# Talking-heads attention and a squared-ReLU feed-forward: the start's gathers on two queues, its loads at once

## The chip, the cores and the metric

One core of one Trainium2 chip. The metric is the device time of one execution in microseconds (us).

## The reference, cut to what matters

```python
scores = scale * np.matmul(q, k.transpose(0, 1, 3, 2))        # 8 batches, 12 heads, 448 x 448
scores = np.einsum('bhij,hg->bgij', scores, w_pre)            # mix the heads
attn = softmax(scores)
attn = np.einsum('bhij,hg->bgij', attn, w_post)               # mix them again
x = np.matmul(attn, v)  # -> 3584 x 768
h = np.maximum(x @ w_in, 0.0)
return h * h @ w_out                                          # 768 -> 2048 -> 768
```

## The kernel before

Scores of one batch are made in four blocks of queries. For each block TensorE writes scores to PSUM (`s_ps`), ScalarE and VectorE evict them to `S` (two buffers, so two blocks). To mix heads with a matmul, the heads must lie along the partitions: a DMA per *tile* of 10 queries gathers 120 rows of `S` into one of twelve `G` tiles. Two tiles are one **double step**: mix (`m_ps`), exponential and sum (`e_sb`, ScalarE), reciprocal (`rc`, VectorE), normalise (`d`, GpSimd), mix back and turn (`at_ps`). TensorE and GpSimd run in the order of the program; the order on the other engines is chosen when the kernel is built.

```python
LAG, AHEAD = 2, 10
gts = [work.tile([P, S], BF16, name=f"G{x}") for x in range(AHEAD + 2)]
for t in gts:
    nc.gpsimd.memset(t[0:OFF, :], 0.0)
...
def gather(k):
    ...
    nc.sync.dma_start(out=g[OFF:OFF + H * n, :], in_=Sb[(b, blk)][x:x + n, :, :])
...
Sb[(b, blk)] = work.tile([P, H, S], BF16, name="S", tag="S", bufs=2)
...
gathers_for(-1)                       # tiles 0 to 9
for n in range(NPAIR, 2 * NPAIR):
    score_pair(n)                     # scores of the second block
for f in loads.get(-1, []):
    f()
for ds in range(nd + LAG):            # one double step
    for i in (2 * ds, 2 * ds + 1):
        for f in loads.get(i, []):    # position i: loads issued by GpSimd
            f()
    ...
```

`w1` (eight loads), `w2` (eight), `v`, `q` and `k` come by DMA from GpSimd, which also converts f32 to bf16 on the way, each at a numbered *position*, two positions to a double step.

The softmax here doesn't subtract the row's maximum and nothing guards it: scores larger than these inputs give would overflow.

## Time and profile before

| | before |
|---|---|
| time, median of three | 623.73 us (622.62 to 626.54) |
| span of the profiled execution | 621.2 us |
| TensorE busy | 557.5 us, 90% |
| gathers | 360, all issued by SyncE |

### The profile page before, as it was taken

The page shows a single profiled execution, that of the slowest core. Times are in us where ns is not written, and L with a number is a line of the kernel's source. Part 1 is how long each engine was busy: PE and PEld are TensorE (multiplying, and loading weights), DVE is VectorE, ACT ScalarE, POOL GpSimd, SP SyncE. Part 2 cuts the span into 40 slices and gives each one's busy share as a digit, 9 for nine tenths or more (in the row PEclk, how much of TensorE's full clock was granted, in tenths as well). Part 3 has the DMA queues.
Part 4 walks back from the last instruction along what each step waited for, and adds up shares of the span by engine and source line. Part 5 has one row for each costly group of instructions (what it writes and reads, how often), then busy time and mean ns, then how long its engine had stood idle before and what let it go on. Part 6 is the DMA issues. An engine that isn't in the chain of part 4 may idle for free.

```text
span 621.2 us, 26855 instructions
## 1 busy us (share of the span) xinstructions
PE 557.5 (90%) x11154; PEld 316.3 (51%) x11154; DVE 431.4 (69%) x1111; ACT 395.7 (64%) x1196; POOL 401.6 (65%) x591
## 2 busy tenths in 40 slices
PE   5545886888899999999999989999999999999997
PEld 3223564654455555554555445554555555555554
DVE  3355997898698768876787768876887787765101
ACT  3445664756677865787568865786578767872320
POOL 8345757647547984699448964699458944893450
PEclk9655989799899999999999999999999999999999
DMA  8799889848945695468753885468544575431102
GB/s 111 127 188 191 139 144 201 132 86 138 190 96 108 105 150 137 110 114 147 152 123 77 136 145 120 112 104 147 140 111 86 86 159 123 88 64 53 39 12 78
DMA packets 90911, 74.10 MB, mean 119 GB/s; under 512 B 6309, under 2 KB 87717, under 8 KB 90789
## 3 DMA queue, kind: packets, MB, share of 16 engines
q1 hardware_dynamic: 51842, 49.57, 33.6%
q0 software_dynamic: 38816, 22.81, 29.0%
q8 instruction: 87, 1.43, 0.9%
q14 instruction: 36, 0.29, 0.1%
q10 hardware_dynamic: 130, 0.01, 0.0%
HBM read 45.63 MB, written 11.01 MB: 91 GB/s over the span
## 4 chain that ended last, share of the span: by engine, by line
PE 65%; POOL 9%; DVE 9%; DMA 6%; ACT 4%; issue 3%; SPq 2%; ACTq 0%; DVEq 0%; POOLq 0%
PE o_ps L267 22%; PE h_ps L234 18%; PE at_ps L368 7%; PE ot_ps L185 7%; DMA G<-S 5%; PE m_ps L337 5%; DVE at L373 4%; POOL d L346 4%; PE s_ps L309 3%; PE tr_ps L162 3%; POOL h L246 3%; SPq L328 2%; DVE S L312 2%; ACT xt L196 1%; ACT e_sb L342 1%
## 5 line engine op out<-in xcount | busy, mean ns | idle before, releaser
L346 POOL TENSOR_SCALAR d<-e_sb,rc 128x448 bf16<-128x448 f32 x360 | 227.2, 643 | 180.0 <-DVE rc L344 178.2
L373 DVE CAST at<-at_ps 112x480 bf16<-112x480 f32 x360 | 219.4, 649 | 46.7 <-PE at_ps L368 43.2
L342 ACT ACTIVATE e_sb<-m_ps 128x448 f32<-128x448 f32 x360 | 195.7, 557 | 25.8 <-PE m_ps L337 12.6
L234 PE MATMUL h_ps<-xt,w 128*128 128x448 bf16 (+2 forms) x960 | 164.4, 319 | 3.2 <-DVE at L373 1.6
L267 PE MATMUL o_ps<-w,h 128*128 128x384 bf16 (+1 forms) x1024 | 162.5, 329 | 0.9 <-ACT xt L196 0.5
L312 ACT CAST S<-s_ps 128x448 bf16<-128x448 f32 x192 | 99.9, 541 | 91.4 <-PE s_ps L309 65.8
L312 DVE CAST S<-s_ps 128x448 bf16<-128x448 f32 x192 | 115.2, 613 | 22.2 <-DMA G<-S 20.1
L234 PEld LDWEIGHTS <-w 128*128 128x128 bf16 x960 | 80.4, 99 | 80.4 <-issue 30.8
L246 POOL TENSOR_TENSOR h<-hr 128x448 bf16<-128x448 f32 (+2 forms) x124 | 109.0, 887 | 17.2 <-ACT hr L244 17.2
L267 PEld LDWEIGHTS <-h 128*128 128x128 bf16 (+1 forms) x1024 | 82.9, 101 | 73.2 <-issue 27.8
L368 PE MATMUL at_ps<-post,d 60*64 60x60 bf16 x5760 | 87.6, 197 | 17.1 <-POOL d L346 9.8
L337 PE MATMUL m_ps<-G,pre 64*64 64x448 bf16 x720 | 79.0, 367 | 22.5 <-ACT S L312 9.6
L368 PEld LDWEIGHTS <-d 60*64 60x64 bf16 x5760 | 65.2, 111 | 61.1 <-issue 24.9
L244 ACT ACTIVATE hr<-h_ps 128x448 f32<-128x448 f32 (+2 forms) x136 | 68.7, 511 | 27.1 <-PE h_ps L234 12.2
L342 ACT ACTIVATION_READ_ACCUMULATOR e_sb<-m_ps 128x1 f32 x360 | 77.8, 216 | 0.0
L344 DVE RECIPROCAL rc<-sm 128x1 f32<-128x1 f32 x360 | 50.2, 155 | 37.3 <-ACT e_sb L342 35.4
L196 ACT ACTIVATE xt<-ot_ps,bvec 128x160 bf16<-128x160 f32 (+3 forms) x144 | 44.7, 384 | 49.2 <-PE ot_ps L185 37.7
L309 PE MATMUL s_ps<-kT,qT 64*64 64x448 bf16 x768 | 70.5, 375 | 0.8
L185 PE MATMUL ot_ps<-at,v 112*64 112x160 bf16 (+4 forms) x1152 | 48.6, 238 | 6.8 <-ACT S L312 4.0
L274 DVE COPY osb<-o_ps 128x384 f32<-128x384 f32 x48 | 25.9, 546 | 40.5 <-PE o_ps L267 40.4
L185 PEld LDWEIGHTS <-v 112*64 112x64 bf16 x1152 | 41.0, 114 | 19.7 <-issue 19.2
L337 PEld LDWEIGHTS <-pre 64*64 64x64 bf16 x720 | 28.0, 109 | 40.6 <-issue 35.1
(39 smaller groups left out, 215.1 us busy)
## 6 DMA issues: line engine op xcount, KB each, us to landing
G<-S SPq DMA_DIRECT2D x352, 105.0 KB
kst<-in_k_dram POOLq DMA_DIRECT2D x24, 224.0 KB, 5.8
qst<-in_q_dram POOLq DMA_DIRECT2D x24, 224.0 KB, 5.3
v<-in_v_dram POOLq DMA_DIRECT2D x24, 224.0 KB, 6.0
w<-in_moe_w_in_dram POOLq DMA_DIRECT2D x8, 384.0 KB, 10.5
w<-in_moe_w_out_dram POOLq DMA_DIRECT2D x8, 384.0 KB, 7.6
out_dram<-osb SPq DMA_DIRECT2D x8, 336.0 KB
out_dram<-osb SPq DMA_DIRECT2D x8, 288.0 KB
```

The costliest lines, as they stand in the source:

```text
L185: nc.tensor.matmul(ps[64 * hh:64 * hh + 64, TW * y + c0:TW * y + 2 + n], lhsT=vs[b][0:PR, g, r, :], rhs=at[0:PR, r, g, c0:2 + n], start=(y ...
L234: nc.tensor.matmul(ps[:, 0:n], lhsT=w1[ft // 4][:, c2, ft % 4 * 128:ft % 4 * 128 + 128], rhs=xts[b][:, c2, c0:c1], start=(c2 == 0), stop=( ...
L244: nc.scalar.activation(out=hr[:, 0:n], in_=ps[:, 0:n], func=ACT.Relu)
L246: square.tensor_tensor(out=h2ts[(b, ft)][:, c0:c1], in0=hr[:, 0:n], in1=hr[:, 0:n], op=ALU.mult)
L267: nc.tensor.matmul(dst, lhsT=h2ts[(b, ft)][:, mt * 128:mt * 128 + ROWS[mt]], rhs=w2[ft // 4][:, ft % 4, n2 * 384:(n2 + 1) * 384], start=(f ...
L309: nc.tensor.matmul(pss[hh][z:z + 64, 0:S], lhsT=qTs[b][rs, p, q0:q0 + 64], rhs=kTs[b][rs, p, :], start=True, stop=True)
L312: copy(out=Sb[(b, blk)][:, 2 * p + hh, :], in_=pss[hh][:, 0:S])
L337: nc.tensor.matmul(pss[y][64 * x:64 * x + 64, 0:S], lhsT=pre[rows, :], rhs=gs[x][rows, :], start=True, stop=True)
L342: nc.scalar.activation(out=e[:, :], in_=pss[y][:, 0:S], func=ACT.Exp, scale=SCALE, accum_out=sm[:, 0:1])
L346: nc.gpsimd.tensor_scalar(out=d[:, 0:S], in0=e[:, :], scalar1=rc[:, 0:1], scalar2=-1.0 / S, op0=ALU.mult, op1=ALU.add)
L368: nc.tensor.matmul(us[x][z:z + 64, c:c + HR], lhsT=d[rows, PR * r + z:PR * r + z + 64], rhs=post[rows, :], start=True, stop=True)
L373: nc.vector.tensor_copy(out=dst, in_=src)
```

## The change

Its intent: issue the first batch's gathers in half the time, have w1 and v loaded before the gathers need the DMA engines, and get the zero fills off GpSimd so that it can issue those loads earlier. The loads of the second batch's q and k and of w2 move up into the room that w1 leaves.

```diff
-        nc.gpsimd.memset(t[0:OFF, :], 0.0)
+        nc.vector.memset(t[0:OFF, :], 0.0)
...
-        nc.sync.dma_start(out=g[OFF:OFF + H * n, :], in_=Sb[(b, blk)][x:x + n, :, :])
+        eng = nc.scalar if b == 0 and k % 2 else nc.sync
+        eng.dma_start(out=g[OFF:OFF + H * n, :], in_=Sb[(b, blk)][x:x + n, :, :])
...
-        for x in range(8):
-            at_load(2 + 2 * (x // 2), load_w1, x)
-            at_load(28 + 2 * x, load_w2, x)
+        for x in range(2):
+            at_load(-1, load_w1, x)
         for x in range(3):
             at_load(-1, load_v, 0, x)
             at_load(44 + x, load_v, 1, x)
+        for x in range(2, 8):
+            at_load(-1, load_w1, x)
+        for x in range(8):
+            at_load(18 + 2 * x, load_w2, x)
         for x in range(6):
-            at_load(14 + 2 * x, load_qk, 1, x)
+            at_load(6 + 2 * x, load_qk, 1, x)
             at_load(46 + 2 * x, load_qk, 2, x)
```

## The prediction

> **What bounds the kernel now.** I read the page's slices first, then the stretches of the start, the chain of waits from 14 to 50 us in order of time, the waits of the same window, and last the trace's DMA packets counted by microsecond. The slices tell where there is time to gain:
>
> ```profile
> PE   5545886888899999999999989999999999999997
> PEclk9655989799899999999999999999999999999999
> DMA  8799889848945695468753885468544575431102
> ```
>
> One slice is 15.5 us. From the eighth on TensorE is nearly always busy, and 95% or more of it from 160 us to 560 us; the change touches nothing there. The first four slices (0 to 62 us) have it half idle at half clock, while the DMA engines are 70 to 90% busy. So the start is the place, and what the start loses or gains is passed on to the end about one for one, since what follows is a full TensorE queue in fixed order.
>
> ```profile
> core 0: us, PE busy (x) PEld busy (x) DVE busy (x) ACT busy (x) POOL busy (x), PEclk, DMA share, GB/s
> 12.00:18.00 6.00, 5.78 (x76) 3.34 (x72) 5.25 (x10) 5.25 (x13) 1.78 (x3) 1.00 0.90 115
> 18.00:26.00 8.00, 4.33 (x54) 1.51 (x52) 3.29 (x10) 3.42 (x12) 3.02 (x5) 0.61 0.56 108
> 26.00:37.00 11.00, 1.23 (x36) 0.68 (x37) 0.49 (x3) 1.22 (x5) 3.14 (x5) 0.50 1.05 180
> 37.00:43.00 6.00, 3.98 (x86) 1.99 (x85) 5.62 (x15) 4.52 (x14) 4.76 (x7) 0.50 0.80 175
> 43.00:54.00 11.00, 4.89 (x131) 2.60 (x133) 6.46 (x19) 4.61 (x16) 6.54 (x11) 0.50 1.13 199
> ```
>
> The third column after the stretch's length is VectorE's, then ScalarE's. Two stretches are nearly dead on every engine (26 to 37 and, in its second half, 43 to 54), and both have the DMA share over 1. Before the first is one with DMA at about half (18 to 26). The chain of waits says who holds whom:
>
> ```profile
> 26.88 1.32 SPq L328
> ...
> 28.38 8.52 DMA G<-S
> 36.90 1.14 DVE S L312 x2
> ...
> 43.82 4.03 DMA G<-S
> ...
> 48.38 4.67 issue
> ```
>
> ```profile
> ACT S L312 <- DMA G<-S: 14.7, 2, 9.8
> DVE S L312 <- DMA G<-S: 13.8, 2, 10.1
> ```
>
> From 17.29 to 28.2 us the chain is SyncE's queue issuing twelve gathers one after the other, 0.77 to 1.32 us each, 11 us in all. Then 8.5 us for gathers to land. The engines waiting are the two that evict scores into S: S has two buffers, so the third block's scores can't be written before all twelve gathers of the first block have left it, and with eight PSUM banks TensorE soon stops too. The second hole (48.4 to 53.3) is the same wait one block later; the 4.67 us that the chain calls "issue" stand beside waits of ACT and DVE that the second view books on the gathers.
>
> Why the gathers are slow to land: the eight loads of w1 (384 KB each) are issued by GpSimd between 24.1 and 42.4 us, into the middle of them. Counted by microsecond, gathers alone move 120 to 157 packets of 896 B (one gather is 120 packets). As w1 comes in, this falls to 28 to 45 a microsecond (26 to 30 us), then 75 to 83 (31 to 37 us), beside some 150 packets of w1. The last gather of the first block, issued at 26.88, lands at 36.8. Meanwhile the queue of loads carried nothing from 18.1 to 25 us, nor for about 1 us at 12 us.
>
> **What the Trainium skill says.** "DMA: Bandwidth & Descriptors", section "Queues, rings and completion order": each DMA engine goes round between the queue rows that have work, a packet at a time, and SyncE and ScalarE have a row each. The trace agrees in that gathers under a load fall to a third or two thirds of their rate, not to nothing. It follows, if it holds, that gathers in two rows get two turns to the load's one. The same page, "Issuing engines are not separate DMA queues", says that a second issuer only saves its sequencer's issue time. Here that time is 0.77 to 1.32 us a gather, which is not small: 11 us of the chain. Which of the two sections describes the gain is open; the kernel before has no run with both rows busy. "VectorE: DVE Perf Modes", "Zero memsets can be issued as uint32 (trn2)": half as many elements for bf16 zeros. The trace agrees in form (pre, 128x64 bf16, is filled as 128x32 uint32 in 85 ns).
>
> **The change part by part.**
>
> 1. The twelve zero fills leave GpSimd, where they stand from 6.18 to 11.18 us (461 ns each, 5.0 us in all). On VectorE as 224 words each I estimate 0.25 us each, 3 us in all, from the 85 ns of a 32-word fill and about 1 ns a word. VectorE is idle 2.06 us before 3.50, 1.33 us before 5.73 and again before its first copy at 7.03. So this costs 0 to 0.3 us on the path, and it frees GpSimd at 6.2.
>
> 2. The w1 and v loads are issued at once. GpSimd begins at about 6.7 instead of 11.7 and 24.1 us. They follow q and k in one queue, which still has these in flight until 11.4, so q and k aren't delayed and the gap at 12 us closes. Amount: w1 3072 packets of 1024 B, at about 165 a microsecond 18.6 us; v 1344 packets of 512 B, at 350 a microsecond 3.8 us. From 11.4 that would end at 34 us alone; with gathers between them I take 35 to 36. In the kernel before w1 ends at about 53. GpSimd will wait for load slots (eight semaphores in rotation) until about 19 us, which is harmless: its first d is at 22.95.
>
> The price: the first gathers, which now run on free engines (first landing about 20.3), run beside v and w1 from the start. At 45 packets a microsecond in each of two rows, about 90 in all, twelve gathers (1440 packets) take 16 us from 16.6, so they land at about 32.5 and not at 36.8. With one row at the later rate of 80, the number is nearly the same, 34.5.
>
> 3. Odd gathers of the first batch go to ScalarE: 22 of them. The first five will stand among its evictions of S at 17 to 19 us; five issues at 0.8 us delay either them or the first exponential (22.0) by 1 to 4 us, I take 2. This lies before the landing of the twelfth gather and so costs nothing extra at the first hole. Later one such issue falls in each step of two tiles. From 60 to 85 us ScalarE is busy 15.6 of 25 us and VectorE 22.8; seven issues of 0.78 add 5.5 us to ScalarE's queue, 84%. It does not become the bound, but its exponentials start later: I take 1.5 us lost.
>
> 4. The loads of q and k for the second batch start 8 positions (four double steps) earlier, those of w2 ten positions earlier. The former now fall into 33 to 45 us instead of 48 to 67, light packets at half the queue's rate. The latter leave the stretch before 101 us, where they were followed at once by v and k and by a gather that stands 6.09 us on the chain (102.27 to 108.36).
>
> Sum. The fourth pair of tiles (m_ps at 37.45) moves to about 33: 4.5 us. The second hole has no w1 any more and two rows: of its 4.7 us I count 4. GpSimd's two w1 issues that stand on the chain at 38.84 (1.5 us) go, and a q or k load comes near: 0.5. At 102 us I count 2 of the 6.09. Less 1.5 for ScalarE. Total 4.5 + 4 + 0.5 + 2 - 1.5 = 9.5 us; I round to 10, which gives 613.7.
>
> **Rivals.**
>
> Rival A, the holes vanish: gathers in two rows run at close to their lone rate, the twelfth lands by 27 us, each double step takes the 2.3 us that it takes between 37.5 and 49, and the eleventh pair, now at 60.86, comes at 47 to 48. With the 2 us at 102 that is 14 to 16 us, or 608 to 610. For it: round turns a packet at a time. Against it: 3.8 MB of loads are in front of the same engines, and the DMA share was over 1 whenever holes occurred.
>
> Rival B, the contention is only moved: the skill's second section is all there is, w1 holds the first gathers as it now holds the later ones, and the first exponential comes at 26 instead of 22. The twelfth gather lands at 35; only the second hole closes. Gain 4 to 6 us, 618 to 620. For it: the fall to 28 to 45 packets as soon as w1 starts.
>
> Rival C, ScalarE becomes the bound: its queue is in order, a gather there waits for S, for a free G and for an earlier gather's semaphore, and everything behind it waits too. If each of 17 later issues holds the exponentials for its whole 0.8 us and no slack takes it up, 13 us are lost and the change is worth nothing: 621 to 628. Against it: a double step takes 2.3 us at the least and some 4 us after 60 us, and the results of an exponential are used two double steps later.
>
> **Range and chances.** My sum lies between A and B. I give A about 0.3, the middle 0.4, B 0.2, C 0.1. Faster by over 2% means under 611.3 us: most of A and a part of the middle, 0.35. Slower by over 2% would take C and a worse schedule of all that follows: 0.03. The range 605 to 621 should hold it 8 times in 10.
>
> **What would show it right or wrong.** Right: the load queue shows no gap from 4 to about 35 us; the hole from 26 to 37 shrinks to under 5 us; that at 48 us is gone; step 3's matmuls stand near 33 us and the first h_ps (62.95) near 53; from 160 us on all stands the same distance earlier. ScalarE's waits on the gathers tell B from A: several microseconds before 35 us and none after would be my middle. It is wrong if first-batch exponentials wait behind ScalarE's DMA issues with TensorE idle after 60 us (C), if q and k land later than 11.4 us, or if TensorE's idle time after 110 us changes by more than 3 us: then the reordered queues, not the loads, would have moved the time.

## More of the kernel before

Columns: out<-in, issuing engine, count, size, median from issue to landing.

```profile
G<-S SPq DMA_DIRECT2D x352, 105.0 KB
kst<-in_k_dram POOLq DMA_DIRECT2D x24, 224.0 KB, 5.8
w<-in_moe_w_in_dram POOLq DMA_DIRECT2D x8, 384.0 KB, 10.5
w<-in_moe_w_out_dram POOLq DMA_DIRECT2D x8, 384.0 KB, 7.6
```

A gather is small against any of the loads, but the loads only have to arrive some time, and a gather has work waiting.

## The result, and the profile after

616.14 us (median of four, 614.33 to 617.23) against 625.13 us before (median of four). Ratios here and below are the mean time of one kernel's fast runs over that of the kernel before in the same rounds, so not quite the ratio of the medians; this one is 0.9854, interval 0.9804 to 0.9904. A second measurement gave 0.9865. So it is 8 to 9 us faster, under 2%, within the range and near the predicted 613.7.

The slices of the changed kernel, to be laid under those of before:

```profile
PE   5456888799799999999999899999999999999997
PEclk9655999999899999999999999999999999999999
DMA  9989958859645885488545875478543565431102
```

The first four slices are no fuller on TensorE than before. Loads stand in the first two slices of the DMA row (9, 9 for 8, 7), as intended, but the start did not get short. The same stretches as in the prediction, now of the changed kernel:

```profile
12.00:18.00 6.00, 5.62 (x70) 2.77 (x69) 5.03 (x10) 3.93 (x8) 2.75 (x5) 1.00 1.31 195
18.00:26.00 8.00, 1.31 (x12) 0.38 (x9) 1.77 (x4) 1.67 (x4) 1.26 (x2) 0.72 1.24 229
26.00:37.00 11.00, 4.52 (x88) 2.04 (x84) 3.70 (x12) 5.17 (x18) 3.10 (x5) 0.50 0.94 202
37.00:43.00 6.00, 4.63 (x118) 2.21 (x118) 5.59 (x17) 4.74 (x16) 5.89 (x10) 0.50 0.88 158
43.00:54.00 11.00, 5.62 (x124) 2.51 (x124) 6.08 (x16) 5.22 (x17) 6.11 (x11) 0.50 1.09 182
```

The hole from 26 to 37 is smaller (TensorE 4.52 us busy for 1.23), but there is a new one from 18 to 26 (1.31 for 4.33), where DMA went from a share of 0.56 to 1.24. One hole was traded for another. ScalarE's stream in order of time shows what the new hole is made of, first in the kernel before:

```profile
14.56 4.47 ACT L312 CAST S<-s_ps 128x448 bf16<-128x448 f32 x10
22.01 0.54 ACT L342 ACTIVATE e_sb<-m_ps 128x448 f32<-128x448 f32 x1 [2.98 <-PE m_ps L337]
```

and in the changed kernel:

```profile
14.62 2.28 ACT L312 CAST S<-s_ps 128x448 bf16<-128x448 f32 x5
16.68 7.61 ACTq L329 DMA_DIRECT2D G<-S  x5
24.33 2.28 ACT L312 CAST S<-s_ps 128x448 bf16<-128x448 f32 x5 [7.43 <-PE m_ps L338]
26.45 0.60 ACT L343 ACTIVATE e_sb<-m_ps 128x448 f32<-128x448 f32 x1
...
27.58 0.80 ACTq L329 DMA_DIRECT2D G<-S  x1
```

In the kernel before, ten evictions of S follow each other from 14.56 to 19.03 and the first exponential is at 22.01. Now five gathers stand among them and take 7.61 us, not 5 times 0.8: four are issued by 20.1, and the fifth has to wait for the semaphore of ScalarE's first gather, which lands at 23.5. The other five evictions, the exponentials and the twelfth gather (27.58) wait behind it. (The view books the 7.43 us before the evictions on a matmul; the fifth issue ends at 24.29, and they begin at 24.33.)

```profile
16.68 7.00 DMA G<-S
...
24.35 2.26 ACT S L312 x5
26.61 0.97 ACT e_sb L343 x4
27.58 6.93 DMA G<-S
...
46.88 3.80 DMA G<-S
```

Those are the chain's long pieces of the changed kernel. The first gather takes 7 us to land, the twelfth another 7, and the second hole is still there, at 46.88. The waits from 16 to 62 us say the same (for 14.7 and 13.8 before):

```profile
ACT S L312 <- DMA G<-S: 9.7, 2, 5.1
...
DVE S L312 <- DMA G<-S: 7.7, 2, 4.3
```

The best single ruler is the start of the first exponential of each double step, since all kernels here do the same work in the same order of steps. In us from the span's start, two profiles of the changed kernel:

```
double step      0      3      8     12     22     23     24     35     60
before       22.01  38.14  54.14  65.04  97.99 100.49 108.85 145.56 215.41
changed      26.45  36.96  52.19  63.08  95.74  98.07 101.31 137.88 207.62
changed (2)  27.04  38.00  53.18  64.07  96.74  99.07 102.31 138.90 206.43
```

The whole start is worth 2.25 and 1.25 us (double step 22). The gain is at one place: from double step 23 to 24 took 8.4 us and takes 3.2, and over the stretch from 22 to 35, 47.6 us become 42.1. After that the kernels run alike: from step 60 to 179, 350 to 352 us. Both profiles of the changed kernel give back some 2 us there (352.4 and 352.2 for 350.1), and both have one window of 3.4 us at half clock, at 352.5 and 351.2 us; of the other profiles only one has such a window (ScalarE's gathers alone, the second profile, 351.9 us).

### The profile page after: what moved, and what is told of

Its sections match the earlier page's. It is cut to its first block, busy times and chain, and to the rows that moved or that the text cites. A ratio compares the mean times of both kernels' runs of the same rounds, so it can differ in the third digit from the quotient of the medians.

```text
span 615.4 us, 26843 instructions
## 1 busy us (share of the span) xinstructions
PE 556.6 (90%) x11154; PEld 313.2 (51%) x11154; DVE 434.4 (71%) x1123; ACT 396.1 (64%) x1196; POOL 397.8 (65%) x579
## 4 chain that ended last, share of the span: by engine, by line
PE 63%; POOL 11%; DVE 11%; DMA 6%; ACT 5%; issue 3%; ACTq 0%; DVEq 0%; POOLq 0%; SPq 0%
PE o_ps L267 22%; PE h_ps L234 17%; PE at_ps L369 7%; PE ot_ps L185 6%; POOL d L347 5%; DVE at L374 5%; DMA G<-S 5%; PE m_ps L338 4%; POOL h L246 3%; PE s_ps L309 3%; PE tr_ps L162 3%; ACT e_sb L343 2%; ACT xt L196 2%; DVE S L312 1%; DVE h L246 1%
## 5 line engine op out<-in xcount | busy, mean ns | idle before, releaser
L374 DVE CAST at<-at_ps 112x480 bf16<-112x480 f32 x360 | 219.5, 649 | 44.9 <-PE at_ps L369 40.8
L234 PEld LDWEIGHTS <-w 128*128 128x128 bf16 x960 | 79.2, 98 | 79.9 <-issue 30.9
L274 DVE COPY osb<-o_ps 128x384 f32<-128x384 f32 x48 | 26.0, 546 | 40.5 <-PE o_ps L267 40.4
L185 PE MATMUL ot_ps<-at,v 112*64 112x160 bf16 (+4 forms) x1152 | 47.3, 234 | 2.8 <-DVE at L374 2.8
L338 PEld LDWEIGHTS <-pre 64*64 64x64 bf16 x720 | 27.9, 108 | 35.5 <-issue 26.5
```

The costliest lines, as they stand in the source:

```text
L185: nc.tensor.matmul(ps[64 * hh:64 * hh + 64, TW * y + c0:TW * y + 2 + n], lhsT=vs[b][0:PR, g, r, :], rhs=at[0:PR, r, g, c0:2 + n], start=(y ...
L234: nc.tensor.matmul(ps[:, 0:n], lhsT=w1[ft // 4][:, c2, ft % 4 * 128:ft % 4 * 128 + 128], rhs=xts[b][:, c2, c0:c1], start=(c2 == 0), stop=( ...
L338: nc.tensor.matmul(pss[y][64 * x:64 * x + 64, 0:S], lhsT=pre[rows, :], rhs=gs[x][rows, :], start=True, stop=True)
L374: nc.vector.tensor_copy(out=dst, in_=src)
```

## The experiments

Twelve runs. The stretches of the ruler for all kernels come after the single runs.

### Putting w2 back in the changed kernel

```diff
-            at_load(18 + 2 * x, load_w2, x)
+            at_load(28 + 2 * x, load_w2, x)
```

> The kernel after, with w2's loads put back ten positions, where the kernel before has them. Theory 1 (most of the gain is not at the start but at 102 us, because w2 is out of the way of v, k, q and the second batch's gathers): the exponential of double step 23 stays near 98 us, that of double step 24 goes from 101 back to 106 or later, and the time is 5 us longer, about 621 us. Rival (the hole at 102 us closes because gathers come earlier against their use, wherever w2 is): double step 24 stays near 101 to 103 and the time at 615 to 617.

619.75 us, ratio 0.9913 (0.9839 to 0.9986). The hole came back: step 23 to 24 takes 7.99 us. The start was 2.4 us better than in the changed kernel (step 23 at 95.7; expected 98), so step 24 was at 103.7 and not 106. Theory 1 holds; the interval of the time alone overlaps that of the changed kernel.

### w2's place alone, on the kernel before

```diff
-            at_load(28 + 2 * x, load_w2, x)
+            at_load(18 + 2 * x, load_w2, x)
```

> The kernel before with w2's loads ten positions earlier, nothing else. If w2's place is worth about nothing in sum (its earlier loads cost at 55 to 85 us what they save at 102 us, as the kernel after with w2 put back suggests: 2.4 us ahead at double step 23, 2.4 us behind at 24, equal at the end): 623 to 626. If the hole at 102 us is a loss by itself: 617 to 620, with double step 24 about 3 us after double step 23 instead of 8.4.

618.13 us, ratio 0.9902 (0.9834 to 0.9971). Step 22 at 97.78 (before 97.99), step 23 to 24 in 3.24 us, step 35 at 139.87 (before 145.56). So a change of one number gives 5 to 6 us, most of what the whole change gives. From step 12 to 22 it costs 0.6 us. How it acts is seen in the stretches around the hole, first before, then this kernel (columns as in the prediction):

```profile
96.00:100.00 4.00, 2.95 (x92) 2.31 (x95) 4.00 (x13) 3.10 (x11) 3.26 (x6) 1.00 1.03 223
100.00:104.00 4.00, 3.26 (x84) 2.25 (x78) 3.50 (x11) 1.62 (x6) 3.97 (x7) 1.00 1.10 209
104.00:110.00 6.00, 1.57 (x26) 1.47 (x27) 1.69 (x4) 1.58 (x6) 2.39 (x5) 0.88 1.20 201
```

```profile
96.00:100.00 4.00, 3.34 (x98) 2.50 (x98) 4.00 (x12) 2.95 (x11) 2.56 (x5) 1.00 0.53 115
100.00:104.00 4.00, 2.94 (x65) 2.23 (x66) 3.97 (x14) 2.64 (x8) 3.94 (x7) 1.00 0.98 132
104.00:110.00 6.00, 5.66 (x158) 4.28 (x158) 5.57 (x17) 5.32 (x20) 5.75 (x9) 1.00 1.22 193
```

From 96 to 100 us w2 still moves in the first (DMA share 1.03), and the last packets of gathers issued then start 6 to 7 us after the issue; the hole follows at 104. In the second only gathers move (0.53), their last packets start about 3 us after the issue, so they are ahead when v, k and q arrive at the same share of 1.22, and nothing stops.

### ScalarE's gathers alone, on the kernel before

```diff
-        nc.sync.dma_start(out=g[OFF:OFF + H * n, :], ...)
+        eng = nc.scalar if b == 0 and k % 2 else nc.sync
+        eng.dma_start(out=g[OFF:OFF + H * n, :], ...)
```

> The kernel before with the odd gathers of the first batch on ScalarE, nothing else. If issue time is what they save: the twelve gathers are issued in about 6 us instead of 11, before w1 begins at 24, so the twelfth lands at 27 to 30 instead of 36, double step 3 is at 32 to 34 instead of 38, the later holes stay, and the time is 3 to 5 us shorter, 619 to 622. If w1 governs all: double step 3 stays at 37 to 38 and the time at 624 to 626.

> ScalarE's gathers alone on the kernel before, once more in five rounds. If the moved loads add nothing to what ScalarE's gathers give: within 2 us of the changed kernel of the same call, ratio 0.984 to 0.990. If the loads carry a part of the gain that adds up: 3 us or more slower than the changed kernel.

615.55 us, ratio 0.9873 (0.9783 to 0.9963), and in five rounds 618.24 us, 0.9898 (0.9860 to 0.9936). Double step 3 at 30.6 and 30.9, better than expected, and step 22 at 90.7 and 90.8: 7.2 us ahead of the kernel before, where the changed kernel, which has this part too, is 1 to 2 ahead. The later hole stays (9.4 and 10.2 us). So the moved loads take away some 5 us of what ScalarE's gathers give at the start and add 5 or more at 102 us. The time of the repeated run is between its two predictions, 2.8 us behind the changed kernel, and the intervals overlap.

It also shows what two issuers are worth. SyncE alone issues gathers at 0.77 to 1.3 us each; two at a time need 0.83 to 1.55 us each here, and up to 2.3 in another run. In the changed kernel, where no gather has moved yet, two at a time need 0.77 to 0.85. The twelfth gather was issued at 23.4 us for 26.9 before, not in half the time, and landed at 27.1 for 36.8. A part of this may be w1's doing: its first load also comes 2.3 us later here (26.4 for 24.1), as GpSimd issues it after its first normalisations.

### All gathers on SyncE, in the changed kernel

```diff
-        eng = nc.scalar if b == 0 and k % 2 else nc.sync
+        eng = nc.sync
```

> The kernel after, all gathers from SyncE again, one row. Theory 2 (two rows give gathers two turns to the load's one, and this is what keeps the start from being worse): gathers move some 64 to 83 packets a microsecond instead of 128 beside w1, the twelfth lands at 38 us or later instead of 34.4, double step 3 starts at 40 instead of 37, and the time is 3 to 5 us longer, 619 to 621. Rival (ScalarE's queue is what hurts the start: its evictions of S stand behind its gathers until 24.3, so the first exponential is at 26.5 instead of 22.0): without them the first exponential is at 24 or earlier, double step 3 at 36 or earlier, and the time is 613 to 615.

616.89 us, ratio 0.9893 (0.9826 to 0.9961). Beside w1, gathers move 80 to 85 packets a microsecond with one row; the changed kernel moves 60 to 68 in each of two, some 127. So theory 2 is right about the rows, and double step 3 is at 40.8 as it said. But only 4 us lie between the two at step 3 and 0.8 at step 22: without ScalarE's gathers its evictions are not held up (first exponential at 24.9 for 26.5), and the second hole is 4.1 us for 7.2. The time fits neither reading, and it doesn't tell the two kernels apart. With w1 in front of the gathers it hardly matters who issues them.

### w1 and v at once alone, on the kernel before

```diff
+        nc.vector.memset(t[0:OFF, :], 0.0)      # for nc.gpsimd.memset
...
-        for x in range(8):
-            at_load(2 + 2 * (x // 2), load_w1, x)
+        for x in range(8):                       # v's three loads after the second
+            at_load(-1, load_w1, x)
```

> The kernel before with v and all of w1 loaded at once behind q and k and the fills on VectorE; gathers, second batch's q and k, and w2 as before. If w1 at once is worth something by itself (it closes the holes at 28 and 48 us): double step 3 at 36 to 39 us, double step 8 at 49 to 51 instead of 54.1, time 617 to 620. If it only moves the contention onto the first gathers: double step 3 at 40 to 41 as with one row and all loads moved, double step 8 at 52 to 54, and the time within 2 us of the kernel before.

620.12 us, ratio 0.9952 (0.9873 to 1.0032). Step 3 is later than before (40.3 for 38.1), as the second reading said, and the second hole is gone (step 7 to 8 in 2.3 us for 6.9), as the first said: 3.6 us ahead at step 22. In the changed kernel that hole is back (7.2 and 6.8 us). What stands in the load queue there, from 47 to 50 us, is q and k of the second batch at 276 to 287 packets a microsecond, and the gathers are down to 26 to 70. This kernel, with q and k in their old place, has none of them until 50. The kernel with all gathers on SyncE is a control for this: until step 8 it differs from this one in the place of q and k alone (its first w2 load is issued at 55.3 us). Its hole is 4.1 us for 2.3, and its step 8 is 2.5 us later. So q and k early cost some 2 us, in one profile of each. They are not the whole of the hole. The other 3 us come with ScalarE's gathers, and kernels that have these gathers with q and k in the old place have a hole of 4.9 to 5.8 us as well (ScalarE's gathers alone, w1 spread). In part this is only that ScalarE's gathers bring step 7 forward by 4.0 us and step 8 by 0.9; the rest stays open.

### w1 back in its old place, all else as changed

```diff
-            at_load(-1, load_w1, x)              # two, then v, then six
+            at_load(2 + 2 * (x // 2), load_w1, x)
```

> The kernel after, w1's loads back where the kernel before has them (v stays, q, k and w2 stay early, ScalarE's gathers stay). Theory 3 (w1 at once puts some 4 us of loads in front of the very first gathers and so costs the start what it saves later): first gather lands near 20 instead of 23.3, first exponential at 22 to 23, the twelfth gather at 27 to 29, double step 3 at 30 to 32 instead of 37; then w1 meets the second block's gathers together with q and k, and of these 5 to 6 us some 2 to 4 are given back; time 611 to 615. Rival (w1 at once is what helps): double step 8 later than in the kernel after (52.2), time 619 or more.

615.25 us, ratio 0.9852 (0.9785 to 0.9918). The first gather lands at 19.8 us and step 3 is at 30.5, as theory 3 says; the first exponential is at 24.1, later than the 22 to 23 expected. The give-back is at the upper end of what was expected: w1, q and k come together, steps 3 to 7 take 16.1 us (8.1 and 8.4 in the changed kernel), and of the 6.4 us gained at step 3 3.9 are given back by step 8, at 49.6. Step 22 is at 93.2. That is 2.6 to 3.6 us ahead of the changed kernel in the profile; the times don't tell the two apart.

One count separates kernels with all of w1 in front from the rest. From the issue of the first gather to the first packet of any gather:

```
w1 all in front:  changed 4.20, 4.15   w2 back 4.18   all on SyncE 4.18   w1 alone 4.17 us
w1 later:         before 1.50   w2 early 1.50   ScalarE alone 1.49, 1.49   w1 back 1.50   w2 early, ScalarE 1.50 us
two of w1 only:   the spread version below 1.95, 1.92   ScalarE from tile 11 1.49 us
```

In the first row v's loads, behind two of w1's, are also still moving, until 20.0 to 20.3 us. In the kernel before they move until 18.8 and its first gather is not held up, so v alone is not the reason. By what path w1 delays a packet in another queue row, the runs don't show.

### w2 early and ScalarE's gathers on the kernel before

```diff
+        eng = nc.scalar if b == 0 and k % 2 else nc.sync
...
-            at_load(28 + 2 * x, load_w2, x)
+            at_load(18 + 2 * x, load_w2, x)
```

> ScalarE's gathers and w2's earlier place on the kernel before, w1, q and k as before. ScalarE's gathers alone left double step 23 at 93.1 and double step 24 at 102.5, a hole of 9.4 us. If w2 in front of v and k makes this hole, it falls to about 3.5 us and the time is 610 to 613. If the earlier w2 delays the start as much, double step 23 is at 96 or later and the time stays at 614 to 617.

618.02 us, ratio 0.9913 (0.9839 to 0.9986): both readings missed. The hole at 102 us closes as expected (3.24 us), but step 22 is at 101.5, later than before. The profiled execution is the slowest of the four (622.39 us). Until double step 7 this kernel does the same as ScalarE's gathers alone and is still 4 us later, since in this execution issues of two queues at once took 2.3 us each; that part is chance. The rest is not: from step 12 to 22, 40.8 us for 34.8 with ScalarE's gathers alone. GpSimd now issues w2 between q's and k's loads while w1 is still coming, and each of those loads takes 14 to 19 us to land. The chain stands on the last of q's: it is issued at 66.05 us (57.7 with ScalarE's gathers alone), TensorE's turns wait for it, and it lands 16.93 us later. Two gains that each hold alone didn't add up, because w1, q, k and w2 stand in one queue in the order of issue.

### w1 spread over the double steps

```diff
+        eng = nc.scalar if b == 0 and k % 2 else nc.sync      # fills on VectorE too
...
         for x in range(3):
             at_load(-1, load_v, 0, x)
+        for x in range(2):
+            at_load(-1, load_w1, x)
+        for x in range(2, 8):
+            at_load(2 * x - 2, load_w1, x)                    # one to a double step
+        for x in range(8):
+            at_load(26 + 2 * x, load_w2, x)                   # 28 before
```

> ScalarE's gathers, fills on VectorE, v and two of w1's loads at once, the other six one per double step, w2 one double step earlier than before. With ScalarE's gathers alone the chain from 25 to 37 us is GpSimd: per double step 1.25 us of d and 1.5 us of issuing two loads. With one issue of 0.75 the step falls from 2.8 to about 2.1 us: double step 6 at 36.5 instead of 38.6 and no later than that at 8 (43), time 611 to 613. If instead the bytes of w1 set the pace there, double step 6 stays at 38 to 39 and the time at 614 to 616.

> ScalarE's gathers with w1 spread over the double steps, once more in five rounds. If w1 at once costs the start 3 us (double step 3 at 31.8 instead of 37.0 in the profiles): 2 to 4 us faster than the changed kernel, 611 to 614. If the profile of 610 us was a lucky execution: 614 to 617, as the changed kernel.

612.57 us, ratio 0.9840 (0.9756 to 0.9924), then 611.51 us, 0.9811 (0.9782 to 0.9840) in five rounds, where the changed kernel had 615.44 us, 0.9865 (0.9830 to 0.9900). It beats both: 4 us faster than the changed kernel and 12.6 faster than the one before (624.11 us in those rounds), which is 1.9%, with an interval that reaches past 2%. The two intervals just overlap; each profile is 6.5 us or more ahead at step 22. Step 6 is at 37.7 and 37.2, short of the 36.5 expected, and step 8 is at 45.9 and 45.4 for the expected 43; steps 3 to 7 take 8.3 and 8.5 us, for 9.6 and 11.0 with ScalarE's gathers alone. Step 22 is at 89.2 and 89.0, 9 us ahead of the kernel before, and the hole at 102 us is 4.4 and 4.6. The same stretches for its second profile:

```profile
18.00:26.00 8.00, 2.42 (x10) 0.73 (x9) 1.75 (x4) 3.06 (x8) 0.00 (x0) 0.59 0.68 168
26.00:37.00 11.00, 8.23 (x202) 4.08 (x202) 8.82 (x26) 8.09 (x27) 10.04 (x15) 0.50 0.88 157
...
43.00:54.00 11.00, 7.52 (x166) 5.33 (x165) 5.41 (x15) 6.76 (x22) 3.94 (x7) 0.52 1.06 191
```

From 26 to 37 TensorE does 8.23 us of work for 4.52 in the changed kernel, at a lower DMA share.

### The changed kernel again

> The changed kernel once more, five rounds, beside the next three on the same chip. Single executions of one kernel differ by 3 to 7 us, so the partial kernels' medians of four (615 to 620) can't be told apart yet. Expected 615 to 617, ratio 0.984 to 0.988, if the first result was typical.

615.44 us, ratio 0.9865, as expected.

### ScalarE only from the eleventh tile on

```diff
-        eng = nc.scalar if b == 0 and k % 2 else nc.sync
+        eng = nc.scalar if b == 0 and k % 2 and k >= 10 else nc.sync
...
-            at_load(2 * x - 2, load_w1, x)      # against the spread version
+            at_load(2 + 2 * x, load_w1, x)
-            at_load(14 + 2 * x, load_qk, 1, x)
+            at_load(18 + 2 * x, load_qk, 1, x)
-            at_load(26 + 2 * x, load_w2, x)
+            at_load(28 + 2 * x, load_w2, x)
```

> As the spread version, but ScalarE takes odd gathers only from the eleventh tile on, so that its first evictions of S and exponentials are not behind gathers, and the six later loads of w1 start two double steps later, q and k of the second batch two later. If ScalarE's queue order costs the first steps 2 to 3 us: first exponential at 22 instead of 25.5, double step 3 at 28 to 30, time 608 to 611. If the start is set by landing gathers anyway: double step 3 at 31 to 33 and the time as the spread version's, 611 to 614; if the later q and k then meet the turns of the second batch, longer.

621.09 us, ratio 0.9930 (0.9896 to 0.9964), a miss. The first exponential is at 22.8, so ScalarE's queue does cost the first steps some 2 us. Step 3 is at 32.05 all the same: its chain is SyncE's serial issue again, then the landing.

```profile
25.74 0.95 SPq L329
...
26.74 4.02 DMA G<-S
```

With w2 at its old place the hole at 102 us is 8.9 us, and q, two double steps later, is waited for by the turns of the second batch. It loses by those, more than by what it tried.

### All kernels on one ruler

First exponential of double steps 3 and 22, and stretches between them, in us:

```
                        step 3  7 to 8  step 22  23 to 24  22 to 35   ratio
before                   38.14    6.94    97.99      8.36     47.57
w1 and v at once         40.26    2.32    94.40      7.63     46.43   0.9952
ScalarE's gathers        30.55    4.92    90.74      9.44     47.88   0.9873
   again                 30.89    4.99    90.80     10.16     48.75   0.9898
changed, w2 back         36.55    5.58    93.36      7.99     45.79   0.9913
ScalarE from tile 11     32.05    5.95    92.57      8.88     47.86   0.9930
spread                   31.78    5.76    89.24      4.40     43.01   0.9840
   again                 31.21    5.74    88.98      4.62     43.32   0.9811
changed                  36.96    7.18    95.74      3.23     42.14   0.9854
   again                 38.00    6.80    96.74      3.24     42.16   0.9865
changed, all on SyncE    40.76    4.06    96.54      3.23     41.60   0.9893
changed, w1 back         30.52    2.97    93.17      3.26     42.12   0.9852
w2 early                 37.27    6.91    97.78      3.24     42.09   0.9902
w2 early, ScalarE        34.28    5.60   101.48      3.24     42.08   0.9913
```

How much of a step's place is chance is seen where kernels are the same program until step 8. The kernel before and w2 early have step 3 at 38.1 and 37.3; the changed kernel, twice, and that with w2 back, 37.0, 38.0 and 36.6, with holes of 7.2, 6.8 and 5.6 us; ScalarE's gathers, twice, and with w2 early, 30.6, 30.9 and 34.3.

The column 23 to 24 sorts the kernels by where w2 is and by nothing else: position 28, 7.6 to 10.2 us; 26, 4.4 to 4.6; 18, 3.2 to 3.3.

## Why the prediction was right, and where not

The time and the range held: 613.7 predicted, 616.1 and 615.4 measured. The sum of 9.5 us is near the 8 to 9 of the timed runs. Its terms are not: in the two profiles the start (step 22) and the hole at 102 us give 2.25 + 5.4 and 1.25 + 5.4 us. The start was counted 5 to 6 us too high and the hole 3.4 too low, and that these nearly cancelled is luck.

- **The first hole, 4.5 us: 1.2 and 0.1 measured at step 3.** The gathers do move at two turns to the load's one where it can be counted directly (32 to 37 us: about 60 packets a microsecond of w1 and of each gather row), and faster than predicted, 127 for 90. Two things were left out. The first packet of a gather starts 4.2 us after its issue when all of w1 is in front, for 1.5 without. And the step "five issues at 0.8 us delay ... by 1 to 4 us ... costs nothing extra at the first hole" failed: ScalarE's queue is held by its fifth gather until 23.5, the first exponential moves by 4.4 and 5.0 us (by 2.9 with all gathers on SyncE, so the held queue is the smaller part of it), and the twelfth gather, which stands behind it, is issued at 27.58 only and lands at 34.5 for the predicted 32.5.
- **The lone rate of gathers was misread.** The 120 to 157 packets a microsecond of the kernel before match the pace of SyncE's issues (120 packets every 0.77 to 1.32 us). Gathers that have piled up and meet no load move at 230 to 285 (all on SyncE, 36 to 38 us). So beside w1 one row (80 to 85) keeps about a third of what it can do. A smaller slip: the load queue was empty from 18.8 to 25.8 us, not from 18.1 to 25.
- **w1 ends at 35 to 36 us: 40.5 and 41.1 measured**, for some 37 with one row. The trace has eleven updates of a gather's semaphore, one soon after the issue (1.1 to 1.6 us in the changed kernel) and ten as it lands, so a gather may run on ten of the 16 DMA engines. An estimate on that footing: w1 alone moves 193 to 199 packets a microsecond (12 to 14 us), and six engines' share of that is 74. Of the 138 that w1 moves beside two rows 64 are left for the ten engines, next to 63 of each row; of the 160 beside one row, 86 next to 82. So equal turns on ten engines fit the counts, as does the later fall of w1 to some 60 once its share on the other six is done. The trace doesn't name engines, so this is not shown.
- **The second hole, 4 us: nothing at the hole itself** (step 7 to 8: 6.9 before, 7.2 and 6.8 after). "Light packets" of q and k were counted as harmless; they were issued at 37.7 to 47.6 us, not 33 to 45, and stand in this hole now. They cost some 2 us of it. The other 3 or so come with ScalarE's gathers, which were counted as a help: with one row the hole was 4.1 us, and 2.3 with q and k left in place too.
- **GpSimd's w1 issues on the chain, 0.5 us: 0.15.** Two issues of k and q, 0.68 us each, now stand on the chain at 41.69 and 43.67 for the two of w1, 1.51 us in all.
- **The hole at 102 us, 2 us: 5.4 measured** over steps 22 to 35. The mechanism was named and right, and its size was off: I counted a third of the 6.09 us, while one number, w2's position, closes the hole in every kernel that has it.
- **ScalarE's issues after 60 us, minus 1.5 us: none.** Steps 10 to 22 take 36.3 us before and 36.0 twice after. Rival C fell there, though with other places of the loads these steps took 38.1 to 44.1 us in single profiles of three kernels with ScalarE's gathers.
- **The fills:** twelve of 245 ns on VectorE (224 uint32 each), 2.9 us, as estimated from 0.25 (0.83 ns a word between 32 and 224 words, for the 1 ns assumed), and TensorE's first matmuls did not move (5.62 us before, 5.65 and 5.75 after).

Of the rivals, B had the start nearly to the number (first exponential 26, measured 26.5 and 27.0; twelfth gather 35, measured 34.5 and 35.5). But the second hole did not close as it said, and the reason that it gave, the skill's second section, is contradicted by the packet counts. Of the signs of being right the first came true, as the load queue has no gap from 4 us on. The others that were specific did not: step 3 is at 37 and 38 us, the hole at 48 us stays, and the first h_ps is at 61.0 and 62.0, not 53. The waits said it too: in the first profile ScalarE waits 4.7 us for gathers after 36 us, where the middle had none. The last sign of being wrong failed in itself: TensorE's idle time after 110 us hardly changed (21.8 and 22.0 us), and yet it was a reordered load, w2, that moved most of the time, just before 110.

What stays open: why ScalarE's gathers go with a second hole (q and k were not put back by themselves in the changed kernel), by what path queued loads delay a gather's first packet, and how much of the differences of 1 to 3 us between partial kernels is chance in issue times.

## What to carry to other kernels

Parts of a change that each shorten the same stretch don't add up; run each alone before crediting the sum to the intent, as here the side move (w2 ten positions earlier) gave most of the gain and the main one (w1 at once), with q and k early, took back most of what the second queue gave at the start. In these runs a bulk load belonged where small latency-bound transfers are not about to start, spread out, and finished well before the next bulk load follows it. On an engine that also computes, an issue that waits on a semaphore holds up everything behind it: here it cost the first exponential 1.5 to 2.8 us, and gathers from two queues still brought step 3 forward by 4 to 7 us.

## What the Trainium skill lacked or had wrong

- "DMA: Bandwidth & Descriptors", "Issuing engines are not separate DMA queues", says that a second issuer only saves issue time. Beside a running load it also changes the share: 80 to 85 gather packets a microsecond with one row, some 127 with two, and w1 down from 160 to 140. The page's own "Queues, rings and completion order" (turns between rows) predicts this, and the measurement agrees with that section.
- The same section calls the issue time usually small relative to the DMA itself. Here it was 0.77 to 1.3 us for a 105 KB gather, while 120 packets at the 230 to 285 a microsecond of piled-up gathers take about 0.5 us. Two issuers at once needed 0.77 to 2.3 us each; no page gives a size for that.
- No page has the delay of a gather's first packet while a long queue of loads stands in another row: first packet 4.2 us after issue with all of w1 queued, 1.5 us without.
- No page has the time of a fill on GpSimd: 4x448 bf16 took 461 ns. What "VectorE: DVE Perf Modes", "Zero memsets can be issued as uint32 (trn2)", says holds: on VectorE the same zeros ran as 224 uint32 in 245 ns.
